# Causal masks of a gated linear attention by ScalarE copies and GpSimd selects in place of VectorE products

## The chip, the cores and the metric

The kernel runs on one core of one Trainium2 chip. A core has five engines that run their own instruction streams and wait for each other through semaphores: TensorE (PE in the profile, its weight loads PEld), VectorE (DVE), ScalarE (ACT), GpSimd (POOL) and SyncE (SP), which here issues every DMA. On-chip data lies in SBUF, the results of matmuls in PSUM. The metric is the device time of one execution in microseconds, the median of several runs.

## What is computed

A recurrent gated linear attention, whose output is the input of a two-layer network with a hardswish gate. All arithmetic is in float32; the weights come as float64.

```python
def _attn_ref(q, k, v, alpha):            # (4, 8, 768, 48) each
    for t in range(S):
        state = alpha[:, :, t, :, None] * state + einsum('bhd,bhe->bhde', k[:, :, t], v[:, :, t])
        y[:, :, t] = einsum('bhd,bhde->bhe', q[:, :, t], state)

def _moe_ref(x, w_in, w_out):             # x (3072, 384), w_in (384, 2048), w_out (2048, 384)
    h = x @ w_in
    g = h * clip(h + 3.0, 0.0, 6.0) / 6.0
    return g @ w_out
```

## The kernel before

The 768 positions of each of the 4 batches are cut into chunks of 128, so there are 24 chunks, numbered through; all 8 heads of a chunk are worked on together, two heads side by side on the 128 partitions. Within a chunk the recurrence becomes matmuls. VectorE scans alpha into running products (step `r` backwards, L311, step `p` forwards, L322) and scales keys and queries by them (`k`, `q`, L334). TensorE multiplies them into scores of key against query, in blocks of two halves of 64 positions (`sc` for one chunk, `sp` for two, L365). Of each 64 x 64 block only the positions where the key is not later than the query may count, so the scores, which lie in PSUM, are multiplied by a constant upper triangular `mask` on their way into the SBUF tile `A` (`m` for one chunk, L375, `mp` for two, L353). The other half of `A` takes the scaled queries for the part that comes from the state (`qa`, ScalarE, L385). TensorE then multiplies `A` with a tile that holds values and state (`ya`, `yb`, L478); ScalarE brings the result into `xT` (`cy`, L487). The state goes its own way: `u` or `up` (TensorE, L452) multiplies keys and values, `sm` (VectorE, L462) adds, `st` (GpSimd, L428) decays the state for the next chunk, `sv` (ScalarE, L438) places it.

The first six chunks are transposed by TensorE (L284). From chunk 6 on VectorE transposes 32 x 32 blocks (`tk`, `tq`, `ca`, L288), and from chunk 8 on two chunks share one group of scores and of state products. There the keys are also turned by VectorE and two DMAs (`kt`, `kw`, `kr`); chunks 6 and 7 have them turned by TensorE (`kb`) and copied by ScalarE (`ck`).

The network works on groups of two chunks, 256 tokens, numbered 0 to 11. Groups 0 and 1 use plain matmuls (`fa`, `fb`, `f`, gate `fr` on ScalarE, product `fg` on VectorE, and `b`). From group 2 the first layer, and from group 1 the second, use fewer products of sums of blocks. In the first layer `xc` are sums of inputs (VectorE, 128 x 128), `M` the 20 products of a group (TensorE, L623, four matmuls each), `n` copies of a product into SBUF (ScalarE, L629), `o` sums of products (VectorE, L560 to L564), `e` the clipped gate (ScalarE, L517), `h` the gate's product (VectorE, L521). In the second layer `s` are sums of hidden blocks (VectorE, L670, L687), `P` the seven products (TensorE, L726, eight matmuls each), `K` copies on ScalarE (L705), `G` the outputs (VectorE, L742, one of four on ScalarE, L739), `O` the stores. Before that the weights have to be rounded from their float64 bits (`w` loads, `d1`, `d2`, `dx` on ScalarE, `d3` on VectorE, L203 to L210, `d4` on GpSimd, L217) and combined into sums (`y` and `x`, VectorE).

All this is issued in one order, written out by hand as a string of words (`run`, at the end of the kernel): `mp.8` is the mask of chunks 8 and 9, `M.9.3` product 3 of group 9, `P.8.2` product 2 of the second layer of group 8; further numbers are buffers or PSUM banks. Every engine executes its own words in the order of the string and waits where a word needs the result of another engine or a buffer that is still read. So a word's place in the string is also its place in its engine's queue, and SyncE issues its DMAs one behind the other in the same way. There are four PSUM banks for the attention and four for the network. `A` has two buffers, one for even and one for odd chunks, both in the tile `both`.

Of the kernel before, what the change touches and what calls it, by code (L numbers as in the profile page):

```python
# [13 lines left out]
ALU = mybir.AluOpType  # L14
# [3 lines left out]
def kernel(  # L18
# [32 lines left out]
    nc = tc.nc  # L51
    B, H, S, D = q.shape
# [4 lines left out]
    NP = H // 2  # L57
# [287 lines left out]
    def masked_two(j):  # L345
        sc = ps_t.pop(("sp", j))
        for c in (j, j + 1):
            A_t[c] = As[c % 2]
        for b in range(2):
            half = slice(HB * b, HB * b + HB)  # L350
            to = both[half, b].rearrange("s c (p a) t -> s a (c p) t", a=2)
            for a in range(2):
                nc.vector.tensor_tensor(  # L353
                    out=to[:, a], in0=sc[a][half].rearrange("s (n t) -> s n t", t=HB),
                    in1=mask[half, half].unsqueeze(1).to_broadcast([HB, 2 * NP, HB]), op=ALU.mult)
# [417 lines left out]
    with tc.manual_schedule():  # L773
# [15 lines left out]
               d4.9 w.12 d2.8 st.4 f.1.1.1 f.1.7.0 sc.4.0.2 f.1.3.3 qa.4.0 d1.8 fr.0.7.0 r.6 d3.8  # L789
               d4.8 d4.4 fg.0.7 m.4 fr.1.1.0 fr.1.7.1 fg.1.7 fg.1.1 d2.10 d1.10 f.1.0.2 d2.12 d3.10  # L790
               r.5 d4.10 fr.1.0.0 fr.1.3.1 fg.1.3 fg.1.0 d3.12 f.1.6.0 f.1.2.1 la.8 lq.5 lv.4.1
               w.11 w.13 lq.6 u.4.1.0 tk.5.3 sm.4.0 sv.4.0 d1.12 qa.4.1 d4.12 fa.4.3 fr.1.2.0
               fr.1.6.1 d2.11 d2.13 f.1.4.2 d1.11 sm.4.1 fg.1.2 k.5 kb.5.1 tq.5.3 d3.11 p.5 d4.11
               tq.6 fg.1.6 q.5 p.6 d3.13 d1.13 st.5 la.7 w.15 lv.5.0 lk.6 w.14 ck.5 b.0.0.1 fb.4
               ya.4.2 qa.5.1 sv.4.1 yb.4 sc.5.0.3 fr.1.4.1 cy.4 u.5.2 b.0.1 f.1.5.0 fr.0.4.0 d1.15
               sv.5.0 qa.5.0 lv.12.1 lk.7 lv.6.2 sv.12.0 sv.6.0 d4.13 xc.2.0 fg.1.4 q.6 xc.2.2
               sm.5.0 fg.0.4 ca.7 tk.6 sv.5.1 d2.15 d2.14 d1.14 d3.15 fr.1.5.1 d3.14 k.6 d4.14
               d4.15 fg.1.5 m.5 b.0.2 b.1.0.2 b.1.1 kb.6.0 ya.5.3 yb.5 b.1.2 cy.5 P.1.0.0 P.1.1.3
               lq.8 K.1.0 ck.6 u.6.2.3 b.1.3 bo.1 b.0.3 tq.7 y.5 y.1 y.3 y.0 y.6 x.0 y.9 y.7 xc.2.1
               y.11 y.13 y.2 y.8 xc.2.3 x.1 s.1.0.0 s.1.1.1 x.2 tk.7 y.10 s.1.2.3 G.1.0.0 y.4  # L800
               sm.6.0 P.1.3.3 xc.2.4 s.1.3.2 P.1.2 sc.6.2.1 y.16 y.12 y.15 s.1.4 r.7 y.17 y.19
               xc.2.5 y.20 s.1.5 xc.2.7 y.14 y.18 y.21 xc.2.6 y.23 lq.9 so.1 lv.7.0 lk.9 bo.0 K.1.2
               K.1.1 P.1.4 M.2.0.1 P.1.5 n.2.0.8 M.2.1 n.2.1.9 G.1.1.1 M.2.7.2 n.2.7.11 sv.6.1
               sm.6.1 k.7 G.1.2.2 xc.2.10 x.3 xc.2.8 p.7 q.7 st.7 y.22 xc.2.9 m.6 M.2.15.3 M.2.2
               n.2.2.10 M.2.8 kb.7.0 M.2.3 M.2.4 P.1.6 qa.7.0 ck.7 n.2.4.12 G.1.3.3 O.1.0 la.9 lk.8
               ca.9 o.2.0.0 M.2.9 u.7.1.2 ya.6.0 e.2.0.0 qa.6.1 yb.6 lv.8.2 cy.6 y.24 r.9 o.2.1.0
               M.2.10 M.2.5 n.2.10.14 e.2.1.1 n.2.5.13 sm.7.0 h.2.0 tq.8 ca.8 tk.8 h.2.1 M.2.6.0
               M.2.11 M.2.18.1 sc.7.0.3 sv.7.1 qa.7.1 n.2.11.15 n.2.18.10 sv.7.0 M.2.12 M.2.16
               M.2.19 n.2.12.12 M.2.13 sm.7.1 r.8 m.7 o.2.3.0 ya.7.3 n.2.13.12 yb.7 cy.7 M.2.14
               o.2.3.1 o.2.4.0 o.2.5.0 o.2.6.0 o.2.2.0 xc.3.1 P.2.0.1 xc.3.3 xc.3.4 e.2.3.0 xc.3.5  # L810
               o.2.2.1 e.2.2.1 M.3.0.0 M.2.17 xc.3.6 k.8 o.2.6.1 xc.3.8 h.2.3 xc.3.0 h.2.2 kt.8
# [144 lines left out]
```

## Time and profile before

| | |
|---|---|
| Device time, median of 3 runs | 529.4 us (529.21 to 529.86) |
| Device time of the profiled execution | 530.19 us |
| Its span in the profile | 528.4 us |
| TensorE clock granted | 1.00 |
| GpSimd busy | 49.7 us, 71 instructions |
| DMA traffic | 54.40 MB, 103 GB/s in the mean |

The span is the time from the first to the last recorded instruction of that execution; the device time has 1.8 us around it. Busy time is the time in which an engine had an instruction in work. A line of the groups reads: source line, engine, operation, output from input, shape and count, then total busy us and mean ns of one, then the engine's idle time just before such instructions and what ended it. One matmul of the source is two instructions in the profile (the four matmuls of an `M` show as x8). The records of VectorE overlap a little: an instruction of 0.68 us is followed by the next after 0.60 us.

### The profile page before, as it was taken

What the parts mean: (1) busy time and instruction counts of PE and PEld (TensorE: products, weight loads), DVE (VectorE), ACT (ScalarE), POOL (GpSimd) and SP (SyncE); (2) the same over time, 40 slices, a digit from 0 to 9 for tenths busy, and PEclk for the clock granted to TensorE, in tenths of its full rate; (3) what the DMA queues carried; (4) which work ended last, traced back from release to release, by engine and by line L of the source; (5) the groups of instructions that cost most, each with busy time, mean ns of one, the idle gap of its engine ahead of it and who ended that gap; (6) DMA issues with size and microseconds to landing.
All of it is one profiled execution on the core that took longest, in us unless ns stands there. A gap on an engine that the chain in (4) does not pass through costs nothing.

```text
span 528.4 us, 15020 instructions
## 1 busy us (share of the span) xinstructions
PE 519.6 (98%) x6300; PEld 495.6 (94%) x6300; DVE 471.7 (89%) x817; ACT 257.9 (49%) x503; POOL 49.7 (9%) x71
## 2 busy tenths in 40 slices
PE   7899999999999999999999999999999999999997
PEld 7788887779999999999999999999999999999997
DVE  6999999999999999999999999999999996276471
ACT  4889866013653643652544536543444545344330
POOL 6323342100000000000000100000000000000000
PEclk9999999999999999999999999999999999999999
DMA  9999987140026535355555453454163150010001
GB/s 173 222 254 265 245 242 170 29 119 1 17 58 140 131 84 120 78 110 125 123 114 133 98 117 75 111 120 118 30 139 92 30 121 13 2 31 8 9 1 45
DMA packets 124100, 54.40 MB, mean 103 GB/s; under 512 B 83328, under 2 KB 116864, under 8 KB 124032
## 3 DMA queue, kind: packets, MB, share of 16 engines
q1 hardware_dynamic: 124032, 53.44, 44.7%
q8 instruction: 49, 0.80, 0.7%
q14 instruction: 19, 0.16, 0.1%
HBM read 44.50 MB, written 8.91 MB: 101 GB/s over the span
## 4 chain that ended last, share of the span: by engine, by line
PE 81%; DVE 12%; ACT 2%; DMA 2%; issue 2%; POOL 0%; SPq 0%; DVEq 0%; ACTq 0%
PE m_ps L726 37%; PE m_ps L623 35%; PE t_ps L478 4%; PE t_ps L365 2%; PE t_ps L452 2%; DVE g_sb L521 1%; DMA rings<-in_alpha_dram 1%; DVE w L208 1%; DVE raw L210 1%; PE m_ps L555 1%; DVE w L207 1%; DVE P L322 1%; DMA qq<-in_q_dram 1%; DVE A L375 1%; PE t_ps L284 1%
## 5 line engine op out<-in xcount | busy, mean ns | idle before, releaser
L726 PE MATMUL m_ps<-w,g_sb 128*128 128x192 f32 x704 | 121.6, 326 | 0.2 <-DVE oh L742 0.2
L629 ACT COPY g_sb<-m_ps 128x512 f32<-128x512 f32 x110 | 63.5, 585 | 115.4 <-PE m_ps L623 95.1
L726 PEld LDWEIGHTS m_ps<-w,g_sb 128*128 128x128 f32 x704 | 113.8, 190 | 1.2 <-DVE oh L742 0.8
L726 PE MATMUL m_ps<-rings,g_sb 128*128 128x192 f32 x528 | 91.6, 326 | 0.8 <-DVE g_sb L670 0.8
L726 PEld LDWEIGHTS m_ps<-rings,g_sb 128*128 128x128 f32 x528 | 85.3, 190 | 1.1 <-DVE g_sb L670 1.1
L623 PE MATMUL m_ps<-xc,w 128*128 128x128 f32 x640 | 83.5, 278 | 0.0
L517 ACT ACTIVATE r<-g_sb,half 128x512 f32<-128x512 f32 x80 | 56.5, 721 | 49.1 <-DVE g_sb L564 22.8
L623 PEld LDWEIGHTS m_ps<-xc,w 128*128 128x128 f32 x640 | 77.8, 192 | 1.5 <-ACT g_sb L629 0.2
L521 DVE SCALAR_TENSOR_TENSOR g_sb<-r,g_sb 128x512 f32<-128x512 f32 x80 | 53.8, 683 | 4.6 <-ACT r L517 4.4
L623 PE MATMUL m_ps<-xT,raw 128*128 128x128 f32 x400 | 52.2, 276 | 0.0
L623 PEld LDWEIGHTS m_ps<-xT,raw 128*128 128x128 f32 x400 | 48.9, 192 | 0.2
L670 DVE TENSOR_TENSOR g_sb<-g_sb 128x512 f32<-128x512 f32 (+1 forms) x55 | 42.1, 792 | 2.6 <-PE m_ps L726 2.5
L428 POOL TENSOR_TENSOR st<-sm,R 128x192 f32<-128x192 f32 x20 | 12.1, 606 | 337.3 <-DVE sm L462 254.6
L623 PE MATMUL m_ps<-xT,w 128*128 128x128 f32 x320 | 41.7, 276 | 0.0
L623 PEld LDWEIGHTS m_ps<-xT,w 128*128 128x128 f32 x320 | 38.7, 192 | 0.2
L385 ACT COPY A<-q 48x256 f32<-48x256 f32 x88 | 35.5, 403 | 6.0 <-DVE q L334 4.7
L560 DVE TENSOR_TENSOR g_sb<-g_sb 128x512 f32<-128x512 f32 x40 | 27.0, 681 | 6.7 <-ACT g_sb L629 6.6
L501 PE MATMUL m_ps<-xT,w 128*128 128x256 f32 x144 | 32.5, 381 | 0.0
L623 PE MATMUL m_ps<-xc,raw 128*128 128x128 f32 x240 | 32.0, 276 | 0.0
L501 PEld LDWEIGHTS m_ps<-xT,w 128*128 128x128 f32 x144 | 26.9, 190 | 3.8
L311 DVE TENSOR_TENSOR_SCAN R<-t,ones 128x516 f32<-128x516 f32 x24 | 29.5, 1230 | 0.6 <-ACT t L302 0.6
L623 PEld LDWEIGHTS m_ps<-xc,raw 128*128 128x128 f32 x240 | 29.7, 192 | 0.2
(105 smaller groups left out, 722.1 us busy)
## 6 DMA issues: line engine op xcount, KB each, us to landing
raw<-in_moe_w_out_dram SPq DMA_DIRECT2D x8, 768.0 KB, 5.9
raw<-in_moe_w_in_dram SPq DMA_DIRECT2D x6, 768.0 KB, 6.3
v<-in_v_dram SPq DMA_DIRECT2D x48, 96.0 KB, 3.2
out_dram<-oh SPq DMA_DIRECT2D x44, 96.0 KB, 2.0
far<-kq SPq DMA_DIRECT2D x64, 64.0 KB, 2.2
kb<-far SPq DMA_DIRECT2D x64, 64.0 KB, 2.1
qq<-in_q_dram SPq DMA_DIRECT2D x36, 96.0 KB, 2.6
aq<-in_alpha_dram SPq DMA_DIRECT2D x36, 96.0 KB, 2.7
```

What stands on the lines that cost most here:

```text
L311: nc.vector.tensor_tensor_scan(out=reverse(R, n - 1, n), data0=reverse(ax, n, n), data1=reverse(ones, n, n), initial=0.0, op0=ALU.mult, op ...
L385: nc.scalar.copy(out=to[:, a], in_=Q_t[j][64 * a : 64 * a + D, :, half])
L428: nc.gpsimd.tensor_tensor(out=st, in0=sm, in1=R_t[j][:, :, 0:1].to_broadcast([C, NP, D]), op=ALU.mult)
L478: nc.tensor.matmul(y_of(j, (i + 1) // 2, p)[:, HB * b : HB * b + HB], vb[:, p, e : e + 32], A_t[j][:, b, 2 * p + a], start=(b == 0 and i = ...
L501: nc.tensor.matmul(h[:, f], w1[:, kk, o : o + C], xT_t[g][:, kk], start=(kk == 0), stop=(kk == KT - 1))
L517: nc.scalar.activation(out=to, in_=h, func=AF.Relu, bias=half, scale=1.0 / 6.0)
L521: nc.vector.scalar_tensor_tensor(out=to, in0=r, scalar=1.0, in1=h, op0=ALU.min, op1=ALU.mult)
L560: eng.tensor_tensor(out=out, in0=in0, in1=in1, op=ALU.add if s1 > 0 else ALU.subtract)
L623: nc.tensor.matmul(acc[g][i][:, f * C : (f + 1) * C], spots[w][:, f * C : (f + 1) * C], x_of(g, x), start=(first and f == 0), stop=last, s ...
L629: nc.scalar.copy(out=slots[z], in_=acc[g][i])
L670: nc.vector.tensor_tensor(out=out, in0=in0, in1=in1, op=ALU.subtract)
L726: nc.tensor.matmul(to[g], a, rhs[:, f], start=(first and f == 0), stop=(last and f == HF - 1), skip_group_check=True)
```

## The change

From chunk 6 on `masked_two` has no product with the mask. ScalarE copies the scores of both chunks out of PSUM into `both`, four copies of 64 partitions x 512 elements; then, once for each half, GpSimd goes over the 1024 elements of its 64 partitions in place and puts zero where the position along the row is smaller than the partition's number. Chunks 0 to 5 keep the product of VectorE, now only as `m`.

```diff
             to = both[half, b].rearrange("s c (p a) t -> s a (c p) t", a=2)
             for a in range(2):
-                nc.vector.tensor_tensor(
-                    out=to[:, a], in0=sc[a][half].rearrange("s (n t) -> s n t", t=HB),
-                    in1=mask[half, half].unsqueeze(1).to_broadcast([HB, 2 * NP, HB]), op=ALU.mult)
+                nc.scalar.copy(out=to[:, a], in_=sc[a][half].rearrange("s (n t) -> s n t", t=HB))
+            at = both[half, b].rearrange("s c h t -> s (c h) t")
+            nc.gpsimd.affine_select(out=at, in_=at, pattern=[[0, 2 * H], [1, HB]], base=0,
+                                    channel_multiplier=-1, compare_op=ALU.is_ge, fill=0.0)
```

The string of words is the same up to its 212th word (`d4.9`) and in another order from there on. `sc.6`, `m.6`, `u.6` and the same of chunk 7 are replaced by `sp.6`, `mp.6` and `up.6`; otherwise the words are the same ones, now and then with another bank or buffer. Some stretches of it:

```diff
-               n.3.11.8 e.3.5.0 M.3.12 n.3.12.10 q.9 O.2.0 kw.9 la.11 kr.8 kr.9 ca.11 up.8.0.1
-               sp.8.2.3 M.3.13 M.3.15.0 M.3.16 G.2.2.0 o.3.3.0 sm.8.0 mp.8 o.3.4.0 sm.8.1 r.10
...
+               y.23 xc.2.0 xc.2.7 qa.7.0 up.6.2.0 sp.6.3.1 M.2.1 M.2.7.2 n.2.1.9 n.2.7.11 M.2.2
...
+               lv.8.2 lv.9.0 O.1.1 sp.8.2.3 M.3.3 M.3.8 M.3.4 e.2.7.0 xc.3.10 G.2.0.1 h.2.5 h.2.7
+               s.2.0.14 s.2.1.11 P.2.3.2 xc.3.9 kt.9 mp.8 st.8 n.3.4.8 o.3.0.0 M.3.9 M.3.5 qa.8.0
...
+               tk.22 o.9.0.0 s.8.2.11 M.9.9 e.9.0.0 qa.21.0 mp.20 k.22 xc.9.9 sm.21.1 h.9.0 st.22
+               kt.22 s.8.3.14 P.8.2 o.9.1.0 M.9.10 n.9.5.12 qa.21.1 K.8.1 ya.20.1 yb.20 ya.21.3
```

In the new string the scores of chunks 8 and 9 stand behind 24 of the products `M` and 9 of the products `P`, in the old one behind 34 and 12. `mp.18` is followed by `n.8.4`, `P.7.2` and `M.8.9` before the first `ya` of its pair, `mp.20` by `P.8.2` and `M.9.10`. The load `w.12` comes later, and the store `so.0` and some of the last `O` stand closer to the end.

More of the change, by code (lines that the diff above doesn't have):

```diff
@@ L794 @@
[L794 to L799, printed above, removed]
@@ new lines @@
+               f.1.6.0 f.1.2.1 lq.6 w.12 d2.12 fr.1.0.0 fr.1.3.1 fg.1.3 fg.1.0 d3.12 tk.5.3
+               fr.1.6.1 qa.4.1 lv.5.0 la.8 lq.5 lv.4.1 sv.4.0 lk.6 w.11 d2.11 fr.1.2.0 d1.11 d1.12
+               ya.4.2 u.4.1.0 fa.4.3 fb.4 lk.7 la.7 lv.6.2 sv.6.0 d4.10 w.13 tk.6 p.5 sm.4.0 k.5
+               kb.5.1 tq.5.3 f.1.4.2 fg.1.6 sm.4.1 fg.1.2 st.5 d4.12 w.15 sv.4.1 k.6 q.5 tq.6 p.6
+               d3.11 d4.11 w.14 sc.5.0.3 yb.4 b.0.0.1 cy.4 fr.1.4.1 qa.5.1 d2.13 ck.5 f.1.5.0 b.0.1
+               u.5.2 qa.5.0 fg.1.4 d2.15 d1.15 d2.14 fr.1.5.1 d1.14 d1.13 fr.0.4.0 sv.5.0 lq.8 m.5
@@ new lines @@
+               d3.13 tk.7 d3.15 q.6 fg.1.5 d4.15 kb.6.0 b.1.0.2 P.1.0.0 b.1.1 ca.8 d3.14 d4.14
+               d4.13 y.5 sm.5.0 fg.0.4 ca.7 sv.5.1 tq.7 b.1.2 ya.5.3 yb.5 b.0.2 P.1.1.3 b.1.3 cy.5
+               ck.6 y.6 s.1.0.0 y.1 y.3 y.0 x.0 xc.2.1 y.9 x.1 s.1.1.1 x.2 y.8 y.2 b.0.3 qa.6.1
+               K.1.0 G.1.0.0 y.10 xc.2.3 y.7 s.1.2.3 y.4 xc.2.4 s.1.3.2 P.1.2 P.1.3.3 y.11 y.15
+               s.1.4 y.16 y.13 y.17 y.12 xc.2.5 r.7 s.1.5 k.7 y.19 xc.2.6 y.20 y.18 p.7 y.21 bo.1
+               lv.7.0 lq.9 so.1 bo.0 K.1.1 P.1.4 K.1.2 P.1.5 kb.7.0 M.2.0.1 ck.7 n.2.0.8 la.9 q.7
@@ new lines @@
+               P.2.6 M.3.14 tk.11 k.11 sm.9.1 ya.8.1 st.10 ya.9.3 yb.8 yb.9 cy.8 G.2.3.3 kt.11
+               o.3.4.0 e.3.4.1 M.3.17 cy.9 la.13 lv.11.0 kw.10 kw.11 lv.10.2 kr.10 tq.11 o.3.6.1
+               h.3.5 M.3.6.3 P.2.5 o.3.2.0 p.10 P.3.0.1 o.3.2.1 h.3.4 xc.4.1 o.3.7.0 xc.4.3 o.3.7.1
+               xc.4.4 G.2.2.0 xc.4.5 M.4.0.0 e.3.2.1 h.3.2 o.3.3.1 xc.4.0 O.2.2 kr.11 lq.12 lk.12
+               sv.10.0 e.3.6.0 e.3.3.1 n.4.0.10 h.3.3 xc.4.6 h.3.6 q.10 xc.4.7 P.3.1.2 M.4.1
+               M.4.7.3 K.3.0 e.3.7.1 p.11 n.4.7.15 n.4.1.13 xc.4.2 s.3.0.9 q.11 h.3.7 G.3.0.0 ca.12
@@ new lines @@
+               s.3.2.12 s.3.1.11 sp.10.2.0 up.10.3.1 M.4.2 P.3.3.2 sm.10.0 lq.13 O.2.3 ca.13
+               sm.10.1 s.3.3.9 xc.4.8 xc.4.10 r.12 P.3.2 qa.10.0 mp.10 K.3.2 n.4.2.14 M.4.3 M.4.8
+               M.4.4 st.11 sv.10.1 qa.10.1 K.3.1 qa.11.0 sm.11.0 s.3.5 P.3.5 qa.11.1 sv.11.0
+               n.4.4.8 sv.11.1 p.12 s.3.4 o.4.0.0 M.4.9 ya.10.3 ya.11.2 yb.10 yb.11 cy.11 cy.10
+               tq.12 xc.4.9 q.12 o.4.1.0 O.3.0 la.14 lk.13 O.2.0 G.3.2.1 M.4.18.2 M.4.10 M.4.5
+               n.4.18.12 n.4.10.9 e.4.0.0 M.4.19 M.4.11 r.13 P.3.4 lv.13.2 O.2.1 p.13 ca.14 tk.13
@@ new lines @@
+               sp.14.2.0 xc.6.9 h.5.2 e.5.6.1 h.5.6 p.16 o.5.7.1 s.5.0.15 sm.14.0 xc.6.7 qa.15.0
+               n.6.0.9 G.4.3.3 M.6.1 P.5.1.0 e.5.7.1 e.5.5.0 h.5.7 h.5.5 sm.14.1 tk.16 sv.14.1
+               n.6.1.13 qa.15.1 K.5.0 G.5.0.1 M.6.2 M.6.7.2 n.6.2.14 n.6.7.8 s.5.1.11 P.5.3.0 M.6.3
+               M.6.4 M.6.8 n.6.4.12 tq.17 tq.16 k.16 O.5.0 O.4.1 sv.18.0 st.15 mp.14 sm.15.0 q.16
+               s.5.2.10 s.5.4 sm.15.1 s.5.3.15 P.5.2 M.6.5 kt.16 o.6.0.0 M.6.9 e.6.0.0 sv.15.0
+               tk.17 sv.15.1 ya.15.0 h.6.0 ca.17 o.6.1.0 r.17 k.17 K.5.1 K.5.2 n.6.5.11 e.6.1.1
@@ new lines @@
+               ya.14.1 yb.14 yb.15 M.6.18.1 M.6.10 P.5.4 kw.16 O.4.2 lv.17.1 la.19 p.17 s.5.5
+               n.6.10.15 M.6.11 P.5.5 ca.18 h.6.1 lv.16.0 O.4.3 st.16 qa.16.1 n.6.18.10 n.6.11.12
+               M.6.19 M.6.12 cy.15 n.6.12.14 cy.14 G.5.1.1 kt.17 P.5.6 M.6.13 o.6.7.0 o.6.5.0
+               M.6.6.1 r.18 G.5.2.3 M.6.15.0 q.17 o.6.3.0 n.6.13.14 M.6.14 o.6.2.0 o.6.2.1 xc.7.1
+               o.6.3.1 xc.7.3 xc.7.4 G.5.3.0 P.6.0.3 qa.17.1 sv.16.0 e.6.2.1 h.6.2 xc.7.5 M.7.0.1
+               xc.7.6 qa.16.0 n.7.0.14 xc.7.2 o.6.6.0 xc.7.0 o.6.6.1 xc.7.7 e.6.6.1 e.6.3.0 p.18
@@ new lines @@
+               xc.7.8 h.6.6 h.6.3 kr.16 lk.18 kw.17 O.5.2 kr.17 up.16.2.3 sp.16.1.0 M.7.1 M.6.16
+               M.7.7.2 n.7.1.10 M.7.2 e.6.5.1 sm.16.0 lk.19 lq.18 sm.16.1 o.6.4.0 M.6.17 st.17
+               sv.16.1 e.6.4.0 n.7.7.13 n.7.2.11 M.7.8 M.7.3 M.7.4 sm.17.0 h.6.4 h.6.5 o.6.7.1
+               ca.19 xc.7.10 P.6.1.0 s.6.0.8 sv.17.1 e.6.7.0 h.6.7 n.7.4.15 K.6.0 qa.17.0 o.7.0.0
+               M.7.9 M.7.5 sv.17.0 mp.16 r.19 s.6.1.9 O.5.1 la.20 O.5.3 G.6.0.0 P.6.3.0 ca.20
+               o.7.1.0 s.6.2.12 s.6.3.8 tq.18 tk.18 n.7.5.9 M.7.10 P.6.2 s.6.5 xc.7.9 s.6.4 tk.19
@@ new lines @@
+               e.7.0.0 n.7.10.12 M.7.18.1 M.7.11 h.7.0 k.19 n.7.11.15 n.7.18.8 K.6.1 e.7.1.1
+               o.7.6.0 ya.17.0 ya.16.2 yb.16 h.7.1 kt.19 yb.17 M.7.12 M.7.19 P.6.4 o.7.7.0 q.18
+               o.7.5.0 k.18 cy.17 n.7.12.11 M.7.13 M.7.15.1 M.7.16 cy.16 e.7.5.0 K.6.2 n.7.13.8
+               M.7.14 P.6.5 o.7.2.0 r.20 kt.18 o.7.6.1 M.7.6.2 G.6.1.2 p.19 P.6.6 o.7.4.0 G.6.2.1
+               h.7.5 P.7.0.0 o.7.2.1 o.7.3.0 xc.8.1 o.7.3.1 e.7.3.1 O.6.0 la.21 kw.19 lq.19 tq.19
+               kr.19 kw.18 O.6.2 xc.8.3 G.6.3.1 e.7.2.0 xc.8.4 xc.8.5 M.8.0.3 n.8.0.11 lv.19.0
@@ new lines @@
+               O.6.1 kr.18 lk.20 xc.8.0 h.7.3 h.7.2 xc.8.7 xc.8.6 q.19 xc.8.8 up.18.1.3 sp.18.0.2
+               M.8.1 M.7.17 M.8.7.2 sm.18.0 ca.21 p.20 sv.18.1 e.7.6.1 h.7.6 o.7.7.1 K.7.0 n.8.1.12
+               M.8.2 P.7.1.1 qa.19.0 e.7.4.1 h.7.4 xc.8.2 s.7.0.14 qa.19.1 n.8.2.9 n.8.7.8 e.7.7.0
+               qa.18.1 M.8.8 M.8.3 tk.20 h.7.7 sm.18.1 st.19 G.7.0.2 s.7.2.13 s.7.1.10 P.7.3.1
+               M.8.4 sm.19.0 sv.19.0 mp.18 n.8.4.15 lk.21 lq.20 tq.20 r.21 O.6.3 lq.21 q.20
+               s.7.3.14 P.7.2 sm.19.1 o.8.0.0 M.8.9 e.8.0.1 sv.19.1 ya.19.1 ya.18.3 yb.18 yb.19
@@ new lines @@
+               st.20 tk.21 k.21 xc.8.10 kt.21 o.8.1.0 M.8.10 M.8.5 e.8.1.0 s.7.5 kw.21 O.7.0
+               lv.20.1 la.23 lv.21.0 sv.20.0 K.7.2 P.7.5 tq.21 xc.8.9 p.21 qa.20.0 n.8.5.13
+               n.8.10.10 M.8.11 cy.19 M.8.18.3 qa.20.1 K.7.1 G.7.2.1 s.7.4 k.20 kt.20 h.8.1 h.8.0
+               cy.18 n.8.11.14 M.8.6.1 M.8.12 n.8.12.9 o.8.3.0 P.7.4 M.8.13 kw.20 kr.21 kr.20 la.22
+               O.7.2 lk.22 n.8.13.15 G.7.1.3 o.8.3.1 xc.9.1 xc.9.3 o.8.2.0 o.8.2.1 P.7.6 M.8.15.1
+               M.8.14 M.8.16 G.7.3.2 n.8.18.9 o.8.6.0 e.8.2.1 q.21 xc.9.4 o.8.6.1 h.8.2 xc.9.5
@@ new lines @@
+               xc.10.3 h.9.2 e.9.3.0 h.9.3 o.9.4.0 xc.10.4 xc.10.10 xc.10.5 P.9.0.3 M.9.17 M.10.0.0
+               P.9.1.1 qa.22.1 qa.22.0 e.9.5.0 e.9.4.1 h.9.5 p.23 h.9.4 e.9.6.0 K.9.0 n.10.0.8
+               xc.10.7 xc.10.6 h.9.6 xc.10.8 q.23 o.9.7.1 e.9.7.1 s.9.0.13 M.10.1 n.10.1.9 O.8.2
+               O.8.3 O.8.1 kr.23 kr.22 up.22.0.2 sp.22.3.1 G.9.0.0 sm.22.0 h.9.7 xc.10.9 s.9.2.10
+               s.9.1.12 M.10.2 P.9.3.1 K.9.2 s.9.3.13 sm.22.1 P.9.2 s.9.5 P.9.5 st.23 sv.23.0
+               n.10.2.14 M.10.3 qa.23.0 sv.22.1 K.9.1 G.9.2.3 s.9.4 M.10.7.1 n.10.7.11 M.10.4
@@ new lines @@
+               M.10.8 n.10.4.15 o.10.0.0 e.10.0.1 h.10.0 sm.23.0 M.10.5 M.10.6.2 M.10.9 P.9.4
+               o.10.1.0 G.9.1.1 M.10.10 n.10.5.15 mp.22 n.10.10.12 M.10.18.0 M.10.11 P.9.6 e.10.1.0
+               n.10.11.10 qa.23.1 G.9.3.2 sv.23.1 M.10.12 n.10.12.13 o.10.3.0 O.9.3 M.10.15.3
+               M.10.16 M.10.13 ya.23.1 ya.22.3 yb.23 yb.22 n.10.13.13 o.10.3.1 h.10.1 o.10.4.0
+               o.10.2.0 M.10.17 M.10.14 o.10.2.1 e.10.3.1 n.10.18.13 M.10.19 P.10.0.2 cy.23 cy.22
+               e.10.2.0 h.10.3 o.10.7.0 h.10.2 o.10.7.1 o.10.6.0 xc.11.1 xc.11.3 o.10.5.0 e.10.7.0
@@ new lines @@
+               h.10.7 o.10.6.1 xc.11.4 P.10.1.3 e.10.5.0 e.10.6.1 h.10.5 xc.11.5 xc.11.0 M.11.0.1
+               xc.11.7 xc.11.6 e.10.4.0 K.10.0 n.11.0.13 h.10.4 G.10.0.2 h.10.6 M.11.7.3 M.11.1
+               s.10.1.14 s.10.0.15 xc.11.8 xc.11.2 P.10.3.0 n.11.7.9 n.11.1.10 M.11.8 M.11.2 K.10.2
+               n.11.2.11 s.10.4 xc.11.9 s.10.3.8 s.10.2.12 s.10.5 P.10.5 M.11.3 M.11.4 n.11.4.14
+               P.10.2 o.11.0.0 M.11.9 o.11.1.0 K.10.1 e.11.0.0 e.11.1.1 O.10.0 O.9.0 G.10.2.0
+               xc.11.10 O.10.2 O.9.1 P.10.4 M.11.10 M.11.5 n.11.10.8 n.11.5.15 M.11.15.0 M.11.11
@@ new lines @@
+               n.11.11.12 M.11.18.1 M.11.16 M.11.12 G.10.1.1 h.11.1 h.11.0 n.11.18.14 o.11.6.0
+               o.11.4.0 e.11.4.1 n.11.12.11 M.11.19 M.11.17 M.11.13 P.10.6 h.11.4 o.11.7.0
+               n.11.13.14 M.11.14 o.11.5.0 o.11.7.1 o.11.3.0 e.11.5.0 e.11.7.1 G.10.3.0 h.11.5
+               h.11.7 o.11.6.1 o.11.2.0 e.11.6.1 h.11.6 s.11.0.11 M.11.6.1 P.11.0.2 K.11.0 s.11.1.8
+               P.11.3.3 s.11.3.9 s.11.2.14 o.11.3.1 o.11.2.1 e.11.3.1 e.11.2.0 P.11.2 h.11.3 h.11.2
+               s.11.4 P.11.1.1 K.11.2 K.11.1 P.11.4 G.11.0.2 s.11.5 P.11.5 O.10.3 O.10.1 so.0
@@ L927 @@
+               G.11.1.0 P.11.6 G.11.2.1 O.11.1 O.9.2 O.11.0 O.11.2 G.11.3.2 O.11.3""")
 _INS = ['q', 'k', 'v', 'alpha', 'moe_w_in', 'moe_w_out']
```

172 lines of the change are left out of this document (45 added, 127 removed).

## The prediction, written before the changed kernel was run

> **What bounds the kernel now.** I read the page first (part 1, the slices, the chain by line), then the busy time by stage, TensorE's waits, the chain in order of time, and last the groups and the timeline around what the change touches. The page (engine, busy us; then slices; then the chain):
>
> ```profile
> PE 519.6 (98%) x6300; PEld 495.6 (94%) x6300; DVE 471.7 (89%) x817; ACT 257.9 (49%) x503; POOL 49.7 (9%) x71
> DVE  6999999999999999999999999999999996276471
> PE 81%; DVE 12%; ACT 2%; DMA 2%; issue 2%; POOL 0%; SPq 0%; DVEq 0%; ACTq 0%
> ```
>
> TensorE is busy for 519.6 of 528.4 us, and its clock row is 9 throughout. The busy time by stage (columns: stretch, PE, PEld, DVE, ACT, POOL busy, clock, DMA share, GB/s) shows that until 450 us VectorE is as full as TensorE:
>
> ```profile
> 75.00:100.00 25.00, 25.00 (x266) 17.55 (x265) 24.66 (x37) 11.47 (x22) 8.41 (x7) 1.00 0.65 152
> 100.00:150.00 50.00, 49.77 (x564) 45.70 (x563) 49.40 (x88) 17.82 (x38) 1.41 (x2) 1.00 0.16 37
> 200.00:250.00 50.00, 50.00 (x589) 49.51 (x588) 49.55 (x85) 22.23 (x48) 0.52 (x1) 1.00 0.49 108
> 450.00:500.00 50.00, 50.00 (x507) 49.79 (x507) 26.39 (x51) 19.11 (x36) 0.00 (x0) 1.00 0.04 13
> ```
>
> So what matters is where one waits for the other. TensorE's waits behind the point where the orders part, and the chain in order of time (start, us, what):
>
> ```profile
> PE m_ps L726 <- DVE g_sb L670: 0.8, 1, 0.8
> PE m_ps L726 <- DVE oh L742: 0.2, 1, 0.2
> ```
>
> ```profile
> 106.57 1.75 DVE rings L670
> 108.32 1.02 DVE k L288
> 110.90 5.47 PE m_ps L726 x32
> 116.99 2.80 PE m_ps L726 x16
> ```
>
> The end is set by VectorE up to 110 us, and by TensorE from 110.9 us to the end. Most that can still be won behind that is those two waits: 1.0 us on PE, 1.9 on its weight loads (1.1 and 0.8); I count 1.4 with the restarts.
>
> **The change part by part.** *The mask.* The groups touched or nearest (busy us, mean ns):
>
> ```profile
> L353 DVE TENSOR_TENSOR A<-t_ps,mask 64x512 f32<-64x512 f32 x32 | 20.6, 682 | 0.4 <-PE t_ps L365 0.2
> L375 DVE TENSOR_TENSOR A<-t_ps,mask 64x256 f32<-64x256 f32 x32 | 12.0, 415 | 0.1
> L629 ACT COPY g_sb<-m_ps 128x512 f32<-128x512 f32 x110 | 63.5, 585 | 115.4 <-PE m_ps L623 95.1 <-DVE g_sb L560 7.0 <-issue 5.3
> masks.py:199 POOL TENSOR_SCALAR_AFFINE_SELECT ident<-ident 128x128 f32<-128x128 f32 x1 | 0.3, 294 | 0.0
> L96 POOL MEMSET v<- 128x1024 f32 x3 | 2.7, 954 | 0.0
> ```
>
> VectorE loses 32 products of 0.682 us and, for chunks 6 and 7, 8 of 0.415: 23.9 us. ScalarE gains 9 pairs x 4 copies of 512 elements out of PSUM, 36 x 0.585 = 21.1 us (from 49% to 53% of the span). GpSimd gains 18 selects of 1024 elements. No row has that size: the select of 128 takes 0.294; with the slope of the memsets (0.205 at 128, 0.954 at 1024) it would be 0.294 + 0.749 = 1.04; with the slope of the two-input sums (L428, 192 elements, 0.515; L217, 768, 1.467: 1.65 ns an element) 0.294 + 1.48 = 1.78. A select reads one operand, so I take 1.1, and keep 1.04 and 1.78. The Trainium skill (GPSIMD Engine Reference, section 3.1) puts a short one-input body at 1.03 cycles an element, by which an estimate for 1024 elements is 0.9 us beside the fixed part; no row here shows that at this size, and the sum would be the same within 0.2.
>
> *The mask's way to TensorE* gets longer: two copies and a select for the first half of a chunk, 2 x 0.585 + 1.1 = 2.3 us, two selects for the second, 1.17 + 2.2 = 3.4, against 2.6 for four products (start to start 0.65). In the new order the tightest pairs (18 and 20) have 3.6 us of TensorE rows (one P of 2.60 and one M of 0.89) between mp and the first ya, and in 18 and 20 ScalarE's last forerunners (sv, and e with qa) hang on matmuls that end some 3 us before mp. Cost 0; uncovered it is at most 1 us in each of the two. Behind mp on ScalarE stand n copies, which free banks that the order uses again over 3 us later; behind the selects on GpSimd stands st, first asked for by the next pair. Both 0.
>
> *VectorE against GpSimd.* This case's timeline shows that they hold each other up (start, us):
>
> ```profile
> 82.15 1.47 POOL L217 TENSOR_TENSOR w<-raw 128x768 int32<-128x768 int32 x1 [0.36 <-DVE raw L210]
> ```
>
> ```profile
> 82.03 0.68 DVE L521 SCALAR_TENSOR_TENSOR g_sb<-r,m_ps 128x512 f32<-128x512 f32 x1
> 82.63 1.53 DVE L334 TENSOR_TENSOR q<-q,P 128x512 f32<-128x512 f32 x1
> 84.09 0.28 DVE L560 TENSOR_TENSOR xc<-xT 128x128 f32<-128x128 f32 x1
> ```
>
> q<-q,P takes both operands from SBUF; it normally takes 0.68 and here 1.53, until after GpSimd's 1.47 us ended at 83.62. L521, with one operand in PSUM, ran beside it untouched. So a select costs VectorE between 0 and its own length; six of ten VectorE steps here (h, s, xc, k, q, the scans) read two SBUF operands, so I take 0.7 for each of the 18: 12.6 us, half of what the masks free. The Trainium skill (SBUF — State Buffer, section "Who interferes with whom") says the same and more sharply: a VectorE instruction with two SBUF inputs and a GpSimd one that reads SBUF exclude each other for a whole instruction, and whichever came first wins. The trace agrees, with 0.85 us lost. By it, read at its worst, the sum is the second rival below.
>
> *The new order.* Both orders are the same up to the gate step at 57.14 us (L521; the next VectorE step starts at 57.76). TensorE is then at 53.8 by the same count (scores of chunk 4 start at 58.98, behind two f steps of 12 x 0.216). So VectorE starts 4.0 us behind, and a step of TensorE is late when VectorE's rows in front of what it needs, plus 4.0, plus what VectorE idles or is held, exceed TensorE's rows. I add up rows, start to start (an L521, L560 or L670 of 512 elements 0.60, a weight rounding d3 2.10, a sum x 1.67, a scan r 1.35 with its reciprocal, p 1.14, a transpose 0.96, xc 0.20, sm and G 0.27; an M 0.893, a P 2.602, an f 2.60, a b 2.59):
> - Before, P.1.3 (at 110.9): 51.9 against 56.9, margin 5.0 - 4.0 = 1.0. TensorE did wait there for some 0.4, so VectorE had idled or been held for about 1.5, of it 0.85 in the row above. Scores of 8 and 9: 112.3 against 119.3, margin 3.0.
> - New, P.1.5: 60.1 against 64.2, margin 0.1. Scores of 8 and 9, which move some 18 us forward: VectorE has 25 y (15.1), 7 d3 (14.7), 4 x (6.7), 15 gate products (9.0), 12 o (7.2), 19 xc (3.8), 6 s (4.7), 5 r (6.8), 5 p (5.7), 11 transposes (10.6), 10 k and q (6.0), and 7 sm, 2 m, 3 G, 1 kt (6.4), sum 96.6, against 100.9 (9 P, 24 M, 8 f, 8 b and the small steps): margin 0.3. Scores of 10 and 11: 134.3 against 140.5, margin 2.2. M.4.18: 148.2 against 157.0, margin 4.8. From chunk 14 on it is over 8.
>
> So what the masks free is spent before 200 us by pulling chunks 8 to 11 forward; the rest comes late, where VectorE has room anyhow. With the same 1.5 of idling and 0.7 a select, TensorE is late by 1.4 at P.1.5, by 1.5 + 1.4 - 0.3 = 2.6 at the scores of 8, by 1.5 + 2.8 - 2.2 = 2.1 at those of 10 and by 0.9 at M.4.18. Lateness stays, so the largest counts: 2.6.
>
> *TensorE's own rows.* Same matmuls, but chunks 6 and 7 together save one turn from large matmuls to small and back: 0.3 us (the first M behind small ones takes 1.16, others 1.06; the gaps at both ends about 0.1 each). *Queues.* w.12 is issued later, and the last stores stand in another order; the last one still follows the last product, and the tail of 2.8 us behind TensorE stays. 0.
>
> **Sum.** +2.6 - 1.4 - 0.3 = +0.9: span 528.4 to 529.3. The profiled execution took 530.19 in all, 0.8 above the median of the three runs; the same 0.9 on the median gives 530.3.
>
> **Rivals.** *First, VectorE gets through in time (faster).* The 1.5 of idling falls away, since an engine that is late does not idle, and the selects of pair 6 fall on its transposes and PSUM steps (11 transposes stand close by): 0.5 late, so 0.5 - 1.4 - 0.3 = -1.2, 528.2; with none late 527.7. For it: by rows alone all margins are positive, and the wait at 370 us (L670) has over 20 us of room in the new order. Against it: the held row above. *Second, the selects exclude VectorE for their whole length:* 1.5 + 2 x 1.1 - 0.3 = 3.4 at scores 8, 1.5 + 4.4 - 2.2 = 3.7 at scores 10, hence +2.0, 531.4; at 1.78 each 6.4 late, +4.7, 534.1. For it: most VectorE steps there read two SBUF operands. Against: GpSimd loses its turn too (L217 stretched from 1.47 to 2.27 at 66.81). It decides from 0.9 held a select on. *Third, the mask comes late:* pairs 18 and 20 at ya, 1 us each, with the first rival's front: +0.8, 530.2. *Fourth, the change doesn't lighten VectorE:* its busy time stays near 470 because held steps count as busy, and the time is as before, 529.4.
>
> **How the numbers follow.** Forecast (late by 1.5 to 3.3) 0.47, first rival 0.27, second 0.14, third 0.05, fourth 0.07. Two tenths of a per cent, about what a measurement of this kernel can tell from no change, are 1.1 us: faster is the first rival but its edge, 0.25; within, the lower half of the forecast, the fourth and part of the third, 0.31; slower, the upper half, the second and the rest, 0.44. The range 527.9 to 533.0 leaves out the first rival's end and the second's; the forecast's own is 529.2 to 531.0.
>
> **What would show it.** L353 leaves VectorE; 36 ACT copies near 0.59; 18 selects near 1.1 (over 1.5 goes to the second rival); VectorE's two-operand steps beside selects stretched; VectorE busy near 460. TensorE idle ahead of the scores of 8 (around 155 us) and of P.1.5 (around 119), none at 370. If TensorE waits at ya for GpSimd, the third rival holds; if no wait behind 58 us is over 0.3, I am wrong and the time is near 528.

## The result and the profile after

| | before | after |
|---|---|---|
| Device time, median | 529.3 us (529.07 to 529.86) | 536.4 us (535.72 to 536.78) |
| Ratio | | 1.0131, interval 1.0113 to 1.0148 |
| Profiled execution: in all, span | 530.19, 528.4 us | 536.49, 534.8 us |

The same kernel, measured once more on another chip, came out at 1.0092 (1.0078 to 1.0106), so the change costs 5.4 to 7.1 us. It is slower by far more than the 0.9 us forecast, and outside the range.

The page of the changed kernel: the line of engine busy times, the VectorE row of the slices, the chain by engine, and the select's group (count, then busy us and mean ns). Lines of the code from L356 on have moved down by one.

```profile
PE 519.9 (97%) x6300; PEld 494.4 (92%) x6300; DVE 455.3 (85%) x777; ACT 275.3 (51%) x539; POOL 71.3 (13%) x89
DVE  7999979999999999999989789889879886375381
PE 66%; DVE 19%; DMA 6%; SPq 3%; ACT 2%; issue 2%; POOL 1%; DVEq 0%; POOLq 0%
L355 POOL TENSOR_SCALAR_AFFINE_SELECT A<-A 64x1024 f32<-64x1024 f32 x18 | 22.7, 1261 | 126.2 <-ACT A L353 117.1
```

TensorE does the same work (519.9 against 519.6 us); VectorE is lighter by 16.4 us, yet its share of the chain rises from 12% to 19%. So the time is lost in waiting, and it is TensorE's. Its waits behind 50 us, those of 0.4 us and more in all (us in all, times, longest):

```profile
PE t_ps L366 <- DVE q L334: 1.7, 1, 1.7
PE t_ps L453 <- DMA kb<-far: 1.1, 2, 0.6
PE m_ps L727 <- DVE g_sb L671: 1.0, 2, 0.7
PE m_ps L624 <- DVE g_sb L561: 0.8, 1, 0.8
PE t_ps L479 <- ACT v L439: 0.5, 1, 0.5
PE m_ps L624 <- DVE g_sb L565: 0.4, 1, 0.4
```

Before, there were two, of 1.0 us together. The new ones lie at many places, each under 1 us but the first (which stands at 79 us, ahead of the first select at 136 us), and none is for the mask (L479 would wait for `A`). One of them, at 373 us, in the timeline (start, us, engine, line; in brackets idle time before, and for what):

```profile
369.52 3.16 POOL L355 TENSOR_SCALAR_AFFINE_SELECT A<-A 64x1024 f32<-64x1024 f32 x2 [1.89 <-ACT A L353]
369.92 1.82 DVE L311 TENSOR_TENSOR_SCAN R<-t,ones 128x516 f32<-128x516 f32 x1
371.73 1.47 PE L727 MATMUL m_ps<-rings,g_sb 128*128 128x192 f32 x8
371.86 1.35 DVE L334 TENSOR_TENSOR q<-q,P 128x512 f32<-128x512 f32 x1
373.14 0.68 DVE L671 TENSOR_TENSOR g_sb<-g_sb 128x512 f32<-128x512 f32 x1
373.87 1.41 PE L727 MATMUL m_ps<-rings,g_sb 128*128 128x192 f32 x7 [0.67 <-DVE g_sb L671]
```

The scan takes 1.82 us (1.22 elsewhere), q<-q,P 1.35 (0.68 elsewhere), both begun beside a select and finished only after it; the sum L671 behind them is late, and TensorE stops in the middle of a product `P`. Adding up, over every VectorE step that overlaps a select, what it took above the median of its form gives 6.05 us, in 8 of 30 steps (this sum is called the time held below). That is near the loss, and is the suspect for the experiments.

### The profile page after: what moved, and what is told of

The parts are those of the page before. It is cut to its first block, busy times and chain, and to the rows that moved or that the text cites. A ratio compares the mean times of both kernels' runs of the same rounds, so it can differ in the third digit from the quotient of the medians.

```text
span 534.8 us, 15031 instructions
## 1 busy us (share of the span) xinstructions
PE 519.9 (97%) x6300; PEld 494.4 (92%) x6300; DVE 455.3 (85%) x777; ACT 275.3 (51%) x539; POOL 71.3 (13%) x89
## 4 chain that ended last, share of the span: by engine, by line
PE 66%; DVE 19%; DMA 6%; SPq 3%; ACT 2%; issue 2%; POOL 1%; DVEq 0%; POOLq 0%
PE m_ps L727 30%; PE m_ps L624 28%; DMA raw<-in_moe_w_out_dram 4%; PE t_ps L479 3%; PE m_ps L513 2%; PE t_ps L453 2%; PE t_ps L366 2%; DVE g_sb L522 1%; SPq L256 1%; DVE g_sb L671 1%; DVE q L288 1%; DVE R L311 1%; DMA raw<-in_moe_w_in_dram 1%; DVE xc L561 1%; DVE g_sb L561 1%
## 5 line engine op out<-in xcount | busy, mean ns | idle before, releaser
L671 DVE TENSOR_TENSOR g_sb<-g_sb 128x512 f32<-128x512 f32 (+1 forms) x55 | 44.4, 830 | 1.1 <-PE m_ps L727 0.9
L355 POOL TENSOR_SCALAR_AFFINE_SELECT A<-A 64x1024 f32<-64x1024 f32 x18 | 22.7, 1261 | 126.2 <-ACT A L353 117.1
L311 DVE TENSOR_TENSOR_SCAN R<-t,ones 128x516 f32<-128x516 f32 x24 | 30.6, 1275 | 0.4 <-ACT t L302 0.4
```

What stands on the lines that cost most here:

```text
L311: nc.vector.tensor_tensor_scan(out=reverse(R, n - 1, n), data0=reverse(ax, n, n), data1=reverse(ones, n, n), initial=0.0, op0=ALU.mult, op ...
L355: nc.gpsimd.affine_select(out=at, in_=at, pattern=[[0, 2 * H], [1, HB]], base=0, channel_multiplier=-1, compare_op=ALU.is_ge, fill=0.0)
L671: nc.vector.tensor_tensor(out=out, in0=in0, in1=in1, op=ALU.subtract)
```

## The experiments

All times are medians beside runs of the kernel before on the same chip; "+1.2" means 1.2 us above those.

**Which part costs: the mask parts, the order, the selects.** The first run keeps the order of before, the second VectorE's products in the new order.

```diff
 # e1: before, with for chunks 8 on
-                nc.vector.tensor_tensor(... in1=mask ..., op=ALU.mult)
+                nc.scalar.copy(out=to[:, a], in_=...)
+            nc.gpsimd.affine_select(out=at, in_=at, ...)
 # e2: after, with VectorE's products in place of copies and selects
 # e4 (and e18): after, with the copies alone
-            nc.gpsimd.affine_select(out=at, in_=at, ...)
 # e7: e1, with the copies alone
```

> The old order with the new mask for chunks 8 on (16 selects, 32 copies). Load theory (the 7 us come from the weight loads of the new order, issued later and one behind the other, and not from the masks): within 0.5 us of before, 529.0 to 530.0. Lock theory (selects hold VectorE up, and TensorE stands behind it): margins of the old order are small as well, so 531 to 533.

> The new order with the products on VectorE kept. Load theory: the stalls ahead of 100 us stay, about 3 us, and the products load VectorE more where it is late, so 533 to 538. Lock theory: the loss goes with the selects, 529.5 to 531.

> The changed kernel without the selects, so that scores of later keys stay in the sums (the zeroing is left out). Lock theory: VectorE is no longer held, TensorE's waits behind 130 us near VectorE's held steps (at 138, 166, 335 and 373 us, together some 2.8 us) shrink, 533.5 to 534.5. Load theory in its pure form: unchanged, over 535.8.

> The order of the kernel before, chunks 8 on with ScalarE's copies and without the selects (the zeroing is left out). With the selects the same order took 537.46 us. If the selects are all of that loss (either theory of them): 528.0 to 529.8 us, as VectorE has 21 us less to do. If the copies on ScalarE come later than VectorE's products did and ya waits for them: 531 to 534 us.

Measured: e1 537.5 (+8.0, 1.0145, 1.0123 to 1.0167), e2 551.2 (+21.7), e4 530.7 (+1.2, 1.0023, 1.0009 to 1.0036), e7 533.1 (+3.7, 1.0069). All theories missed e1 and e2, and e4 came out lower than any had it; e7 lies in its second case. The new order without a lighter VectorE overloads it, as TensorE's longest waits in e2 show:

```profile
PE m_ps L726 <- DVE g_sb L670: 6.1, 5, 2.4
PE m_ps L623 <- DVE g_sb L560: 6.0, 4, 2.4
PE m_ps L726 <- DVE oh L742: 2.0, 1, 2.0
```

In the old order the new mask costs at two places. Copies alone: ScalarE's other work (copies of products, `qa`) stands behind them. With selects too, `ya` waits for the mask itself. TensorE's waits in e7, then the longest in e1:

```profile
PE m_ps L621 <- ACT g_sb L627: 1.3, 3, 0.7
PE t_ps L476 <- ACT A L383: 0.7, 1, 0.7
```

```profile
PE t_ps L479 <- POOL A L355: 3.0, 6, 1.0
PE m_ps L727 <- DVE g_sb L561: 1.5, 1, 1.5
```

So each part costs more without the other; and of what both cost, e4 gives the selects some 5.7 us (536.4 against 530.7; 4.2 by the second measurement, 5.4 less 1.2), and the rest 1.2. In the two profiles part of the 5.7 arises ahead of the first select, as the section on adding up shows, so 5.7 may be too much for the selects.

**Held, or a longer way?** A select can cost by holding VectorE, or by the mask reaching `ya` later. e10 lets the selects write aside, so that `ya` waits for the copies alone; e11 doubles them behind the finished mask.

```diff
 # e10
-            nc.gpsimd.affine_select(out=at, in_=at, ...)
+            aside = raws[2]...[half, 2 * QB : 3 * QB].bitcast(bfloat16)...
+            nc.gpsimd.affine_select(out=aside, in_=at, ...)
 # e11: after, and behind both selects of a pair
+        for b in range(2):
+            nc.gpsimd.affine_select(out=aside, in_=both[half, b]..., ...)
```

> The changed kernel, but each select reads the mask's tile and writes (as bfloat16) to a third of a staging tile that nothing reads any more; the zeroing is left out. It repeats the run with the selects aside, whose place turned out to hold weights. Theory 'held' (VectorE stands still beside the selects): 534.5 to 537.0 us. Rival 'longer way' (the mask comes later to ya): 530.3 to 532.0 us.

> The changed kernel with two more selects behind those of each pair, which read the finished mask and write (as bfloat16) to that same unused third: the computation is whole, GpSimd's selects double. Theory 'held': 539.5 to 542.5 us. Rival 'longer way': 536.0 to 537.5 us.

Measured on one chip with the changed kernel itself (e9, +5.4): e10 535.5 (+5.8), e11 541.0 (+11.2, 1.0210, 1.0196 to 1.0224). The longer way is worth nothing in the new order that these runs can tell, and double the selects cost about double. By the count used above VectorE is held 7.1 us in e9's trace and 13.1 in e11's: 6.0 more held. The medians differ by 5.9 us, but the profiled executions only by 3.2, as e9's was its slowest (537.8); from the first select on e11's TensorE loses 5.1 us more, of it 1.3 at one `ya` behind GpSimd's longer queue. The selects written aside took as long as the others:

```profile
L357 POOL TENSOR_SCALAR_AFFINE_SELECT raw<-A 64x1024 bf16<-64x1024 f32 x18 | 22.6, 1255 | 126.4 <-ACT A L353 125.8
```

A first pair of such runs, e5 and e6, wrote to the first two thirds of that tile:

> The changed kernel, but each of the 18 selects reads the mask's tile and writes its result to a tile that nobody reads, so the zeroing is left out: GpSimd does the same work at the same places, and ya waits for the copies alone. Theory 'held': the selects cost their 5.7 us because VectorE's steps stand still beside them; that stays, so 535.5 to 537.0 us. Rival 'longer way': they cost it because the mask reaches ya later; that is gone, so 530.5 to 532.0 us. Between the two: both, in the shares that the time shows.

> The changed kernel with two more selects behind the two of each pair, of the same size, that read the finished mask and write to a tile that nobody reads: GpSimd's work doubles, the mask is ready when it was. Theory 'held': another 4 to 6 us, 540 to 542.5 us. Rival 'longer way': the mask is as late as before, 536.0 to 537.5 us (at most st behind the selects comes later).

They came out at 533.4 (+3.9; one of six executions, the profiled one, took 1878 us) and 540.3 us (+10.8), but are not used: that part of the tile holds sums of weights by then, so selects and products could wait for each other.

**What holds VectorE.** Each select became a memset of the same tile, with the same waits ahead of and behind it.

```diff
-            nc.gpsimd.affine_select(out=at, in_=at, ...)
+            nc.gpsimd.memset(at, 0.0)
```

> The changed kernel with each select replaced by a GpSimd memset of the same 64x1024 elements, which waits for the same copies and is waited for by the same matmuls, but reads nothing; the scores of chunks 6 on become zero, so that part of the computation is left out. Its length, by the memset row of the page, is 0.95 us against the select's 1.14. Theory 'the read port' (VectorE's steps with two SBUF operands are held only by GpSimd instructions that read SBUF): no step beside a memset is stretched, VectorE busy near 450 us, 530.3 to 531.8 us. Rival 'any GpSimd instruction': VectorE busy 454 to 456 us, 533.5 to 536.5 us.

> The changed kernel without selects once more (the zeroing left out), as the zero for the run with memsets on the same chip: 530.0 to 531.5 us by either theory.

Measured: 531.8 us (+1.3, 1.0020, 1.0000 to 1.0040), beside 531.1 (1.0024, 1.0000 to 1.0048) without any (e18). The same place in its timeline:

```profile
364.99 0.94 POOL L355 MEMSET A<- 64x1024 f32 x1 [1.87 <-ACT A L353]
365.44 1.16 DVE L311 TENSOR_TENSOR_SCAN R<-t,ones 128x516 f32<-128x516 f32 x1
366.13 0.95 POOL L355 MEMSET A<- 64x1024 f32 x1 [0.19 <-POOL A L355]
366.72 0.67 DVE L334 TENSOR_TENSOR q<-q,P 128x512 f32<-128x512 f32 x1
367.30 0.69 DVE L670 TENSOR_TENSOR g_sb<-g_sb 128x512 f32<-128x512 f32 x1
```

Beside a memset the scan is not held at all (1.16 against 1.82), and in the whole trace no step that overlaps a memset is longer by more than 0.25 us. A memset differs from a select in more than the read (it is another operation, and 0.95 us long against 1.14), but in the kernel before the integer sums of L217, which read as well, held VectorE too. So it is the read of GpSimd's instruction that holds. The Trainium skill (SBUF — State Buffer, section "Who interferes with whom") states just this: a VectorE instruction with two SBUF inputs contends with a GpSimd instruction that reads SBUF, not with one that only writes it. The traces agree on both halves, with 6.05 us and none.

**Do the holds add up?** The forecast let only the largest lateness count and gave the selects from chunk 14 on over 8 us of room. Two runs have selects in the early or in the late pairs alone, and one takes the product of the timeline above out of the way of its selects.

```diff
 # e13 / e14
+            if j < 14:        # e14: j >= 14
                 nc.gpsimd.affine_select(out=at, in_=at, ...)
 # e16: after
-    ... mp.18 n.8.4.15 lk.21 lq.20 tq.20 r.21 O.6.3 lq.21 q.20 s.7.3.14 P.7.2 ...
+    ... mp.18 n.8.4.15 lk.21 lq.20 s.7.3.14 tq.20 r.21 O.6.3 lq.21 q.20 P.7.2 ...
```

> The changed kernel with selects for the pairs 6 to 12 alone; the zeroing of chunks 14 to 23 is left out. VectorE's held time in the changed kernel's trace is 3.7 us beside these pairs (0.9, 1.9, 0.9, 0) and 2.4 beside the others (0.4, 0.7, 1.3, 0, 0). Theory 'each hold counts' (VectorE has no store of lead to pay from): 530.7 + 3.7 = 534.4 us, taken as 533.5 to 535.0. Rival 'the largest lateness counts' (the prediction's step; late selects are free): 535.2 to 536.8 us.

> The changed kernel with selects for the pairs 14 to 22 alone; the zeroing of chunks 6 to 13 is left out. Theory 'each hold counts': 530.7 + 2.4 = 533.1 us, taken as 532.2 to 534.0. Rival 'the largest lateness counts' (over 8 us of room there): 530.2 to 531.2 us.

> The changed kernel with the same sum s.7.3.14 moved ahead of tq.20, r.21 and q.20, so that it no longer stands behind the two VectorE steps that the selects of pair 18 hold by 1.3 us. Theory 'each hold counts where a product waits behind it': the wait of 0.83 us at 373 us goes and the time falls by that, 534.2 to 535.9 us. Rival (the hold costs the same at the next product behind): a wait of 0.6 to 1.3 us shows up within the next 15 us, time as before, 535.0 to 536.8 us. The profile decides, not the time.

Measured beside 530.4: e13 533.8 (1.0073, 1.0048 to 1.0098), e14 534.3 (1.0070, 1.0045 to 1.0094), e16 535.2 (1.0089, 1.0064 to 1.0115). Less the 1.2 of e4, the early selects cost 2.2 us and the late ones 2.7 (each within about 1.5), held time 3.7 and 2.4. So the late selects are not free, and no single lateness decides: the rival misses both runs (e13 lies in the range of the theory, e14 0.3 us above it).

The profiles say it more sharply. All these kernels have e4's order of TensorE's work, so each weight load can be set beside the same one in e4's trace, and the difference is how far TensorE is behind. What it loses from the first select to the end, beside the time held in the same trace (us):

| | after | e3 | e9 | e10 | e11 | e13 | e14 | e16 | e17 (memsets) |
|---|---|---|---|---|---|---|---|---|---|
| held | 6.05 | 5.3 | 7.1 | 6.0 | 13.1 | 3.7 | 2.4 | 6.5 | 0 |
| lost from the first select on | 3.4 | 2.7 | 5.3 | 5.8 | 10.4 | 3.6 | 2.0 | 4.7 | 0.9 |

So half to all of the held time comes through, and the 0.9 of e17, where nothing is held, is about what this comparison can't tell. In the first profile another 2.5 us were lost ahead of the first select; that the time held comes so near the whole loss there is thus in part luck. The 0.9 us held beside pair 10 (at 204 us) cost TensorE nothing there.

e16's timeline:

```profile
366.91 2.77 PE L727 MATMUL m_ps<-w,g_sb 128*128 128x192 f32 x16
368.18 2.68 POOL L355 TENSOR_SCALAR_AFFINE_SELECT A<-A 64x1024 f32<-64x1024 f32 x2 [1.89 <-ACT A L353]
368.42 1.44 DVE L671 TENSOR_TENSOR g_sb<-g_sb 128x512 f32<-128x512 f32 x1 [0.71 <-PE m_ps L727]
370.41 2.77 PE L727 MATMUL m_ps<-rings,g_sb 128*128 128x192 f32 x16
372.91 0.68 DVE L561 TENSOR_TENSOR g_sb<-m_ps,g_sb 128x512 f32<-128x512 f32 x1
373.65 1.16 PE L624 MATMUL m_ps<-xc,w 128*128 128x128 f32 x8 [0.47 <-DVE g_sb L561]
```

The wait inside `P` is gone (16 matmuls in one piece at 370.41), and a wait of 0.47 us has come at the next product, for the next sum: the rival of that run, with a shorter wait than its 0.6 to 1.3. The line of 368.42 shows why. The sum, moved ahead, first waits 0.71 us for TensorE, then is itself held (1.44 against 0.68). VectorE can't run ahead here, since what it sums are TensorE's products; 5 us later TensorE waits for it. In e4 the same sum ends at 367.45, the second half of its `P` starts at 366.69 + 1.47 = 368.16: the lead is 0.7 us, not 8.

**The early waits and the weights.** By the starts of its matmuls, the profile above has 2.9 us of TensorE's waits between 62 and 81 us, ahead of the first select. e3 puts the loads w.12 and w.11 earlier; e9 is the changed kernel again; e12 has the order of before up to cy.4.

```diff
 # e3: after, w.12 directly behind d4.9, w.11 between lq.5 and lv.4.1
 # e12: words of the order before up to cy.4, then after's order of the rest
```

> The changed kernel with two loads moved forward: w.12 directly behind d4.9, where the old order has it, and w.11 ahead of lv.4.1 in place of behind lk.6. Load theory: ScalarE's wait of 5.6 us for the load at 72 us and TensorE's wait of 1.7 us at 79 us go, 2.5 to 3.1 us faster than the changed kernel, 533.3 to 533.9. Lock theory: no change, 536 to 536.8.

> The changed kernel once more, for a second profile of it. Its first one shows 2.9 us of TensorE waiting between 62 and 79 us, ahead of the first select, which two other kernels with the same early order do not show. If that is part of the change: 2 to 3 us of waits there again. If it belongs to that one execution (a slow landing of a weight): under 1 us there, and the waits behind 135 us grow by as much, since the time is again 535.5 to 537.0 us.

> The changed kernel with the order of the kernel before up to cy.4 (some 80 us, weights w.12 and w.11 where they were) and its own order from there. Theory 'early queues' (the new places of w.12 and w.11 cost the early waits): 533.0 to 534.2 us. Theory 'held': 535.5 to 537.0 us, the early waits of the one profile are taken up by VectorE's lateness behind it.

Measured: e3 536.1 (+6.6), e9 535.1 (+5.4), e12 536.0 (+6.2). Neither move of the weights gains anything that these runs can tell. In the profiles the early waits vary: 1.3 us in e9 (between its two cases), none over 0.2 in e11, whose order is the same. They are not the main cause, since e10 and e11 lose 5.8 and 10.4 us without them; but in the first profile they are 2.5 of the 5.9 us that it lies behind e4's, and how much of the time between executions of this kernel (534.2 to 537.8 in e9) they make stays open.

**Versions that might have won.** e8 gives only pair 18 to ScalarE and GpSimd, where TensorE's one long wait of before stands; e15 only puts the sum it waits for ahead of the four products.

```diff
 # e8: before
+                if j == 18: nc.scalar.copy(...)          # and the select
+                else: nc.vector.tensor_tensor(...)
 # e15: before
-    ... o.8.1.0 mp.18 s.7.3.14 sm.19.0 ...
+    ... o.8.1.0 s.7.3.14 mp.18 sm.19.0 ...
```

> The kernel before, with copies and selects for chunks 18 and 19 alone, where its one long wait of TensorE (0.9 us at 369 us, for L670 behind the four mask products) stands. Theory 'held': two selects hold VectorE at most 1 us against 2.6 that the products took, so the wait shrinks: 528.4 to 529.3 us. Rival 'longer way': the wait is replaced by one at ya of 1 to 2 us: 529.6 to 531.0 us.

> The kernel before, with one word of the order moved: the sum s.7.3.14 ahead of the four mask products of pair 18 in place of behind them. TensorE's one long wait (0.9 us at 369 us) was for that sum. If the sum's operands are there in time and the mask has the room: the wait goes, 528.4 to 529.0 us. If the mask, 0.7 us later, is late at ya in its place: 529.2 to 529.8 us.

Measured: e8 530.2 (1.0011, 1.0001 to 1.0021), e15 531.1 beside 530.4 (1.0015, 0.9998 to 1.0031). Both remove the wait at 369 us, and neither is faster. In e8 the mask takes its place, at `ya`, as that run's rival had it, though for 0.44 us and not 1 to 2; what keeps e15 from gaining stays open:

```profile
372.72 1.10 PE L485 MATMUL t_ps<-A,v 128*32 128x64 f32 x64 [0.44 <-POOL A L361]
```

No version that was run beats the kernel before.

## Why the prediction was wrong

**Right.** The prices: a copy took 0.580 us (0.585 forecast), a select 1.14 in the median (1.1). VectorE lost its products and is busy 455 us (near 460). The mask's longer way costs nothing in the new order (e10), though it does in the old one (e1, e8). The direction was that of the largest case, and the main cause, VectorE held by selects beside steps with two SBUF operands, is the one that the forecast's largest term named.

**Mis-sized, too high.** "I take 0.7 for each of the 18: 12.6 us". Held were 6.05 us, 0.34 a select: many steps beside selects are transposes or read PSUM. A step that is held waits for the whole rest of the select, as in the second rival, but only 8 of 30 are.

**Wrong, and the main error.** "Lateness stays, so the largest counts: 2.6", with margins added up from a common start ("From chunk 14 on it is over 8"). The margin of a sum of rows is a lead only if VectorE may run on. It may not: its sums wait for TensorE's products, so at the product that was looked at it is ahead by 0.7 us (at 368 us), where the rows sum up to over 8. (The other leads were not measured; the one behind pair 10 took a hold of 0.9.) That VectorE makes up little, because its next input comes only after TensorE has moved on, is argued, not shown. What is shown is that holds add up, early and late (e13, e14), and that of 5 to 7 us held 2.7 to 5.8 come through. "None at 370" failed for the same reason: TensorE waited 0.67 us at 373. The two places of the lateness were wrong as well: at P.1.5 (122 us) TensorE waited 0.34 us for a forecast 1.4, and ahead of the scores of 8 (159 us) not at all. Added up, the 6.05 us held on top of e4's 1.2 give 529.3 + 7.25 = 536.6, against 536.4 measured, but that close a hit is in part luck, as the table shows; the forecast's own 12.6, added up, would have given 529.4 + 12.6 - 1.4 - 0.3 = 540.3.

**Wrong, small.** "Queues ... 0." Without selects the new order still takes 1.2 us more (e4), and TensorE waits for keys read back from DRAM, which it does nowhere behind 50 us in the trace before (e15's, in nearly that order, has one such wait, of 0.7 us). The changed kernel, at `up.18`:

```profile
357.59 0.26 PE L453 MATMUL t_ps<-v,kb 64*48 64x48 f32 x2 [0.61 <-DMA kb<-far]
358.37 0.83 PE L453 MATMUL t_ps<-v,kb 64*48 64x48 f32 x54 [0.53 <-DMA kb<-far]
```

By the rows of TensorE's work between the words, kr.18 and kr.19 stand 10.9 and 5.5 us ahead of up.18 in the old order, and 0.1 and 1.0 in the new. The forecast followed w.12 and the stores past SyncE's queue, but not these reads. That the wait goes when they are moved back was not tried, so what makes up the 1.2 us is argued.

**The removed wait** (-1.4) was only moved: at 370 us of before stands one product's late sum, and so it does at 373 us of after. **The second rival** came nearest, with the right exclusion but the wrong way of adding: its 531.4 and 534.1 also let one lateness count.

## What to carry to other kernels

Work moved to GpSimd isn't free for VectorE: count the VectorE steps with two SBUF operands that will stand beside each GpSimd instruction that reads SBUF, and charge the rest of that instruction to each. Where two engines feed each other at every step, a margin added up over a long stretch is no store; take the lead at the single product, and add the delays up rather than take the largest (the sum is an upper estimate: here half to all of it came through). After a reordering, check for each read that a DMA fetches how much of the bound engine's work is left between its issue and its use.

## What the runs showed of the hardware

The hold goes both ways: selects took 1.14 us where nothing contended and up to 1.96 behind a held scan, while memsets of the same tile took 0.95 throughout. In this program SyncE's queue also waits for landings: in the changed kernel its loads of keys, queries and alpha (L264) stood for 5.4 us in three waits for weight loads of 768 KB to land. In the trace the DMAs take eight completion semaphores in turn, and the load that waited 3.4 us has that of the weight load eight places ahead of it. The longest waits of SyncE between 50 and 100 us:

```profile
SPq L166 <- POOL w L217: 8.2, 4, 4.2
SPq L264 <- DMA raw<-in_moe_w_out_dram: 5.4, 3, 3.4
SPq L274 <- DMA raw<-in_moe_w_out_dram: 2.8, 1, 2.8
```
